# A fifteen-product scheme for the first matmul, with all orders of work laid out anew

## The chip, the cores and the metric

The kernel runs on one core of a Trainium2 chip. The metric is the time on the device, in microseconds (us), from launch to end. Every figure in the profile comes from one profiled execution. PE is TensorE's matmul, PEld its weight load, DVE is VectorE, ACT ScalarE, POOL GpSimd, SP SyncE, whose queue starts most DMAs.

## What is computed

An attention block with a decaying state (RWKV-6) for 4 batches, 8 heads, 768 steps and head size 48, and on its output a two-layer network with an exact gelu:

```python
for t in range(S):
    cur = np.einsum('bhd,bhe->bhde', u[None] * kt, vt)
    y[:, :, t] = np.einsum('bhd,bhde->bhe', rt, state + cur)
    state = wt[:, :, :, None] * state + np.einsum('bhd,bhe->bhde', kt, vt)
...
x = attn_out.transpose(0, 2, 1, 3).reshape(B * S, H * D)   # 3072 x 384
h = x @ w_in                                               # w_in 384 x 2048
g = 0.5 * h * (1.0 + erf(h * inv_sqrt2))
return g @ w_out                                           # w_out 2048 x 384
```

All of it is float32 on the chip.

## The kernel before

**Tiles.** The 3072 rows are worked in eight tiles of 384 (half a sequence of one batch). For tile x, `attention(x)` leaves the transposed rows in `xT` (128 partitions x 3 chunks of d_model x 384 tokens), and `mlp(x)` makes h, the gelu and the output from it. While `mlp(x-1)` runs, attention x is finished and attention x+1 begun. Attention's matmuls are 64x64 and come in bursts; its masks, products and states are DVE's, its copies into `a_sb` ACT's.

**Who sets the order.** Nothing is scheduled by a tool: the program is recorded in the order in which it is written out, and each engine works its own instructions in that order. Two tables hold the order. `PLAN[x]` is a string with a letter per step: "." is the next step of `mlp(x-1)`, "s" of attention x, "f" of attention x+1, "l" of the loads, "c" of the conversion of the weights, "w" of sums of weights, "x" of sums of tokens. `ORDER[x]` lists the steps inside `mlp(x)` for tiles 1 to 7. Tile 0 is computed plainly (`h_plain`, `g_plain`; lines 1121 and 1133), since the sums of weights are not there yet.

**The first matmul before.** h has 16 blocks of 128 rows, 3 chunks of d_model and 2 halves of 192 tokens: plainly 96 products of 128x128 by 192 columns. `h_ops` takes four steps q, each with four row blocks (2 from each half of h). Letters A to G add products into a PSUM bank (`two`, line 1043 issues them), with sums of weights (`s(1)` to `s(4)`) and of tokens (`t1` to `t4`, `l01`). Chunks 0 and 1 take seven products where eight would be plain, chunk 2 goes plainly. Small letters read a bank: "a" copies it into a second one (line 1091), "b", "d", "i", "j" are gelus (1072), "e", "f" copies into `g` (1104, 1106), "c", "g" saves into `o_sb` (1076), "k", "l" add a save to `g`, by an accumulating DMA from POOL's queue (1081) or for the last q by DVE (1083). The sums of weights are in `h_sums` (lines 1010 to 1018, in two parts, during tiles 0 and 1), those of tokens in `sums_of_x` (line 1029, five per tile).

**The second matmul**, `g_ops`, takes twenty products of four 128x128 by 192 each ("=" in the order), with sums of g by DVE ("+", line 1157), banks filled with zeros by ACT ("<", 1167) and ends ("!") by ACT (1188) or DVE (1190); the last ones store the rows. The change leaves its tables as they are.

**PSUM.** From tile 1 on, the first matmul has four banks: two of the tag "mm" (`bank`, `h_ps`) and two of "u" (`bank_u`, `u_ps`); attention has two pairs of banks (`pair`). A matmul that adds to a bank must wait until ACT has read it.

**Loads and conversion.** The weights come as float64 and are made float32 by ACT (lines 432 to 435) and DVE (440, 443). `rkw` comes through SP's queue.

Of the kernel before, what the change touches and what calls it, by code (L numbers as in the profile page):

```python
# [10 lines left out]
F32 = mybir.dt.float32  # L11
# [10 lines left out]
C = 64  # L22
G = 64
D = 48
# [16 lines left out]
        ".lls.....sslsc.lsslll.sl.sls..sl.lscsl..sss.lscs.lscs.s.clll.s..s.cccsss...wss..ss.ff"  # L41
    ),
    1: (
        "c.ccc.clccs.cc..csscc...wcsc.csc.s.c.ccsc.scl..c..csclwccs.ccc.sc.cccs..ccs.c..csss.c...s.ccss.scl.l"
        "wccc..ll.csccl.ccclcc.cfc.cwfwf..wcw.sfff...ff.w....lww.fff.fsfx.xfx..w.w.....w.f..f.cw.f..xx.."
    ),
    2: (
        "ss.w.s.sswssw.s.s....s...slsl.s.s.sw..ww.ss.w..sw...sw.ss..w......swws.ss..s.s..s.sss.l.wsw..s..ss.."
        ".s..l....ls.w..sw..s...w.s....ss.ssww.s..w.s...s.s.s..s.sl.s.......s.s.l........s..ls.s......s...l.."
        "f...ls...f..ff....fx.xx....ff.xffx"  # L50
    ),
    3: (
        ".................l...l...ss..s..ss...s.lsss..s..sss.s.s.sss..s..s.s.s......s.ss.ss.ss..s..ss.sss..ss"
        ".ss.s....l.sl..ss.....s.......ss.s.s..ss..s.s.ss..s.s...s......s.s...l....ssss..l..s.s.l..s.ls.f...f"
        "......lfxx.xx..x"
    ),
    4: (
        ".s.ss.l.......s.s............s....sl..s....sssss..s.ss..ss..s..ss......s.s..ssss..ss.sl..s..s..s.s.s"
        "s.s.....s.ss.ssss..ss.s.lss..ss.s..s.....s.s.l.s.s......sss.....ss.....ss..s...s.ssl..s..s...llsls.f"
        "....s.....f.l..fxx.xxx"  # L60
    ),
    5: (
        "...ss..ss.s..ss....s..s................l..ss.l.....s.slss.ss...s.ss.s....ss.s..s...sssss.sss..ss..s."
        "s....s...ssss.sss..s...ssss....s....ssss...s....sls.sssss..s..s........l.....s.....s..ssls..sl..ls.l"
        ".sf....f.f.f...lxxxx.x."
    ),
    6: (
        "...s...s.s.ss.s...s............l.s.....s...ss...ss....s.ss.s..ss..ssslss...s.s...ss.s.s...l.s.sl..ss"
        "s.s...s.s.ss..ss.s.s.sss..s.s...ss..s.ssss..sss...l..s...s.s..ss.s..........s....sl......ss.ls.l.lfs"
        ".s.ff.f....f..l..xx.xfffffffxx"  # L70
    ),
    7: (
        "........................s.s....sssss.s......sss.ss...ss.s...ssss..ss..s.s...ss.ss.....s..s.ss.s..s.s"
        "ss.s...s....s..s......s.s......s.....s..ss.ssss..s.ssss...s........s..s.s.s.s.s....s.......xx....xxx"
    ),
}

# [22 lines left out]
        "E0 e0 A0 a0 C0 c0 F0 B0 A1 b0 a1 E1 B1 F1 f0 e1 f1 k0 G0 G1 b1 g0 D0 A2 d0 a2 C1 l0 B2 g1 i0 c1 E2 e2 F2 "  # L100
        "C2 D1 j0 b2 l1 c2 d1 A3 k1 f2 G2 a3 g2 j1 k2 l2 i1 E3 e3 F3 f3 D2 C3 +22 c3 G3 g3 B3 =a +e5 D3 d2 <i l3 "
        "b3 d3 <g j3 j2 k3 i2 i3 +23 +03 +e0 =i =b +e1 =g =j +01 +e2 =k !b !k !g +e3 !a +E2 +E3 =h !j =c =m !h "
        "+00 =q !m +20 !c <p +E0 +e4 !q =l +E4 =n !l !n =s =p =o !s !p =f =t !f !o =r !t =d =e !r !d !i !e"
    ),
    2: (
        "A0 E0 a0 B0 F0 e0 b0 C0 A1 f0 a1 c0 G0 B1 g0 F1 E1 b1 f1 D0 e1 k0 C1 d0 !i c1 A2 a2 k1 G1 A3 i1 B2 g1 l0 "
        "b2 F2 i0 f2 D1 d1 a3 !b G2 j0 E2 l1 F3 B3 e2 C2 g2 b3 l2 c2 E3 j1 f3 G3 e3 C3 +22 g3 +e5 D2 l3 k2 j3 c3 "
        "d2 D3 i2 d3 =b j2 <g =a <i k3 +03 =g i3 =k =i +e0 +01 +00 +23 !k =j +e1 +e3 +20 !g =h !j +e2 +E3 +E2 =c "
        "!h !d =m +e4 !m !c =q <p +E0 =p =l !p !q =n !l +E4 !n =s !s =f =o !f =t =r !o !t =d =e !r !e !a"
    ),  # L110
    3: (
        "A0 E0 a0 B0 e0 b0 C0 A1 c0 F0 E1 a1 e1 f0 B1 b1 G0 A2 F1 g0 D0 C1 k0 l0 d0 f1 c1 a2 G1 F2 E2 g1 B2 k1 e2 "
        "D1 !a b2 f2 E3 d1 C2 e3 j0 c2 l1 A3 G2 a3 F3 j1 C3 k2 g2 !b i0 f3 D2 l2 d2 G3 g3 i1 D3 c3 k3 B3 <i l3 "
        "+22 d3 j3 b3 i3 j2 <g =i =a =g !d =b +03 =k i2 +23 +e0 +e5 !g +01 +e1 +e2 =j +e3 =h +E3 =c !k !h !j +00 "
        "!i +E2 =m +20 +E0 !m =q =l !q +e4 +E4 !l !c =n =s <p =p !s !p !n =o !o =f =t !f =r =d !t !r =e !e"
    ),
    4: (
        "A0 E0 a0 B0 e0 F0 b0 C0 f0 A1 G0 c0 E1 k0 a1 B1 g0 F1 e1 D0 b1 A2 l0 f1 C1 G1 d0 a2 g1 l1 B2 c1 b2 E2 D1 "
        "e2 F2 A3 f2 C2 j0 j1 d1 c2 a3 k1 k2 G2 F3 g2 i0 E3 f3 D2 i2 B3 e3 G3 l2 i1 g3 D3 d2 C3 b3 +22 <i l3 +e5 "
        "j2 j3 +e2 c3 d3 =i <g =b +03 +23 =g =a =k k3 !g =j +e0 i3 =h !d !k !j +01 !a =c +e1 +E2 +e3 +E3 !i +00 "  # L120
        "!h =m +20 !c !m +e4 =q <p !q =l +E0 !l +E4 =p =n =s !n !p !s =o !o !b =f =d !f =t =r !t !r =e !e"
    ),
    5: (
        "A0 E0 a0 F0 e0 B0 C0 b0 A1 f0 a1 G0 F1 g0 l0 f1 B1 c0 E1 e1 G1 b1 D0 C1 g1 k0 d0 A2 a2 c1 D1 !b E2 d1 B2 "
        "b2 l1 i0 F2 e2 C2 j0 k1 i1 c2 f2 A3 a3 G2 k2 F3 E3 g2 f3 D2 G3 d2 e3 l2 g3 j1 C3 i2 c3 B3 D3 +22 <i l3 "
        "!i k3 d3 =b <g j3 j2 +03 =g b3 +23 =i +e0 i3 !a =a +e5 +01 !g =k =h =j +e1 !k !j +e3 !h =c +e2 +E3 +E2 "
        "=m =q !c +00 !m !d +20 !q =l <p +e4 !l +E0 =p =n +E4 !p =s !n =o !s !o =t =f !f =d !t =r =e !r !e"
    ),
    6: (
        "A0 a0 E0 e0 F0 B0 C0 b0 A1 f0 G0 a1 c0 E1 B1 e1 k0 F1 C1 f1 c1 b1 G1 g0 k1 E2 A2 !a D0 d0 e2 g1 C2 l0 a2 "  # L130
        "c2 D1 d1 B2 A3 l1 b2 a3 F2 E3 f2 F3 !i j1 G2 i1 g2 B3 j0 f3 e3 !d i0 +22 D2 b3 l2 G3 +e5 +e2 k2 !b i2 g3 "
        "C3 D3 c3 l3 j3 d3 d2 <g =a =b j2 =g <i k3 +23 +03 +e0 i3 !g =k +01 =h +00 +E2 !k +e4 =i =c =j +e1 +E4 "
        "+20 !h =q +E0 !j +e3 +E3 !q !c =m !m <p =l =p !l =n =s !p !s !n =o =f !o !f =t !t =r =d =e !r !e"
    ),
    7: (
        "A0 a0 E0 e0 B0 b0 F0 f0 A1 a1 C0 c0 k0 G0 g0 l0 B1 b1 E1 e1 F1 f1 D0 d0 i0 A2 a2 j0 C1 c1 k1 G1 g1 l1 B2 "
        "b2 E2 e2 F2 f2 D1 d1 i1 A3 a3 j1 C2 c2 k2 G2 g2 l2 B3 b3 E3 e3 F3 f3 D2 d2 i2 G3 g3 l3 j2 C3 c3 k3 =a !a "
        "D3 d3 i3 j3 +22 +e5 =b !b <i +e2 =i !i <g +03 =g !g +23 +e0 +e1 =k !k +e3 +01 +E3 +E2 =j !j +00 =h !h "
        "+20 =c !c +e4 =m !m +E0 +E4 =q !q =l !l =n !n =s !s <p =p !p =f !f =o !o =t !t =r !r =d !d =e !e"
# [9 lines left out]
def kernel(  # L149
# [295 lines left out]

    xT_of, done, behind, ready = {}, set(), set(), set()

    def attention(x, unit):
# [14 lines left out]
        if x not in xT_of:  # L463
            xT_of[x] = wk.tile([128, NJ, T], F32, name="xT")
# [431 lines left out]
        for i in range(NI):  # L896
            for p in range(2):
                for b in range(np_):
                    q, c3 = divmod(i, N3)
                    for g in range(2):  # L900
                        c = 2 * c3 + (p + g) % 2
                        src, c0 = (st, c - 1) if c else (before, NC - 1)
                        if src is None:
                            continue
                        o = ((parts[b] * Q + q) * NC + c0) * D
                        nc.tensor.matmul(ys[b][0][c % 2][half[g ^ swap(b)], i * C:(i + 1) * C],  # L906
                                         lhsT=src[half[g], o:o + G], rhs=rc[half[g], b, i, c % 2],
                                         start=False, stop=True, skip_group_check=True)
        if split:
# [8 lines left out]
        for b in reversed(range(np_)):  # L918
            for q in reversed(range(Q)):
# [11 lines left out]
                ysb = wk.tile([128, T], F32, name="ysb", bufs=1)  # L931
# [48 lines left out]
    HK = HF // 2  # L980
    s_of, x_sums, s12_of = [], [], {}

    def homes():
# [9 lines left out]
        second = [more[1][:, i * WI:(i + 1) * WI] for i in range(HK)]  # L993
        third = [s_home[:, i * WI:(i + 1) * WI] for i in range(HK)]
        fourth = [z[:, FG * 128:] for z in spare]
        s_of.extend((second, third, fourth))

    def h_sums(k):

        if not k:  # L1000
            homes()

        def w(a, c, k):
            return w_in_sb[:, a * HK + k * 2:a * HK + k * 2 + 2, c, :]

        def pieces_of(i, k):
            return s_of[i - 2][2 * k:2 * k + 2]

        for i in range(2):
            nc.vector.tensor_sub(pieces_of(3, k)[i], w(0, 0, k)[:, i], w(1, 0, k)[:, i])  # L1010
        yield
        nc.vector.tensor_add(w(1, 0, k), w(1, 0, k), w(1, 1, k))
        yield
        for i in range(2):
            nc.vector.tensor_sub(pieces_of(2, k)[i], w(1, 0, k)[:, i], w(0, 0, k)[:, i])
        yield
        for i in range(2):
            nc.vector.tensor_sub(pieces_of(4, k)[i], w(0, 1, k)[:, i], pieces_of(2, k)[i])
        ready.add(k)
        yield  # L1020
# [301 lines left out]
```

## Time and profile before

| | us |
|---|---|
| median of 3 runs (583.15 to 585.53) | 585.1 |
| the profiled execution | 583.43 |
| its span, first to last instruction | 581.7 |
| first h product of tile 0 | 46.1 |
| first work of tile 1's part (banks cleared, L208) | 125.2 |
| first h product of tile 7 | 522.4 |

The windows below give us for the stretch, then the busy time of PE, PEld, DVE, ACT and POOL with the number of instructions, the granted clock, the share of DMA and its GB/s. The rows are ten-microsecond stretches of the start and of the turn from tile 0 to tile 1:

```profile
0.00:10.00 10.00, 7.68 (x114) 3.58 (x114) 5.27 (x29) 3.08 (x5) 5.10 (x16) 1.00 0.78 262
10.00:20.00 10.00, 6.51 (x246) 4.71 (x246) 9.79 (x22) 3.57 (x5) 2.86 (x5) 1.00 0.69 210
20.00:30.00 10.00, 8.27 (x233) 5.17 (x233) 7.70 (x16) 3.88 (x7) 0.00 (x0) 0.84 0.61 192
90.00:100.00 10.00, 10.00 (x81) 6.23 (x74) 9.36 (x29) 8.24 (x9) 0.00 (x0) 1.00 0.22 85
```

The groups of the profile give line, engine, operation, shapes and count, then the busy time, the mean time of one in ns, and how long the engine was idle before them. A float32 product is two matmul instructions. An instruction's own time includes the part in which the next one already runs, so the time that a product takes from PE is read from the distance of starts.

```profile
L1043 PE MATMUL h_ps<-xT,w_in_sb 128*128 128x192 f32 x560 | 109.7, 328 | 0.0
L1121 PE MATMUL h_ps<-xT,w_in_sb 128*128 128x384 f32 x96 | 33.2, 494 | 0.0
L1091 ACT COPY u_ps<-h_ps 128x384 f32<-128x384 f32 x28 | 13.1, 468 | 35.8 <-PE h_ps L1043 25.1
```

### The profile page before, as it was taken

The page shows a single profiled execution, that of the slowest core. Times are in us where ns is not written, and L with a number is a line of the kernel's source. Part 1 is how long each engine was busy: PE and PEld are TensorE (multiplying, and loading weights), DVE is VectorE, ACT ScalarE, POOL GpSimd, SP SyncE. Part 2 cuts the span into 40 slices and gives each one's busy share as a digit, 9 for nine tenths or more (in the row PEclk, how much of TensorE's full clock was granted, in tenths as well). Part 3 has the DMA queues.
Part 4 walks back from the last instruction along what each step waited for, and adds up shares of the span by engine and source line. Part 5 has one row for each costly group of instructions (what it writes and reads, how often), then busy time and mean ns, then how long its engine had stood idle before and what let it go on. Part 6 is the DMA issues. An engine that isn't in the chain of part 4 may idle for free.

```text
span 581.7 us, 17597 instructions
## 1 busy us (share of the span) xinstructions
PE 567.2 (98%) x7544; PEld 510.4 (88%) x7544; DVE 453.0 (78%) x880; ACT 290.2 (50%) x634; POOL 58.8 (10%) x63
## 2 busy tenths in 40 slices
PE   7789999999999999999999999999999999999997
PEld 3476666669999999999999999999999999999997
DVE  6878967989889978688887979789788988730171
ACT  2468987134762358235672357324671357425520
POOL 3100000003100030003100120003100021002200
PEclk9999999999999999999999999999999999999999
DMA  6669833222451442345223631526314242212401
GB/s 241 200 193 334 275 111 110 70 79 37 68 130 54 112 85 41 95 127 93 29 39 99 171 43 15 126 70 163 43 28 106 94 56 29 43 39 42 54 1 41
DMA packets 61853, 55.07 MB, mean 95 GB/s; under 512 B 32336, under 2 KB 46928, under 8 KB 61776
## 3 DMA queue, kind: packets, MB, share of 16 engines
q1 hardware_dynamic: 50256, 45.62, 26.1%
q0 software_dynamic: 11424, 8.26, 10.9%
q8 instruction: 59, 0.97, 0.7%
q14 instruction: 18, 0.15, 0.1%
q10 hardware_dynamic: 96, 0.07, 0.0%
HBM read 36.24 MB, written 4.72 MB: 70 GB/s over the span
## 4 chain that ended last, share of the span: by engine, by line
PE 94%; DVE 2%; DMA 1%; issue 1%; ACT 0%; SPq 0%; DVEq 0%
PE u_ps L1043 33%; PE h_ps L1043 19%; PE o_ps L1043 13%; PE h_ps L1121 6%; PE o_ps L1133 5%; PE d L689 5%; PE d L550 4%; PE kv_ps L817 2%; PE y_ps L906 2%; PE y_ps L859 2%; DMA rkw<-in_rkw_dram 1%; PE warm L324 1%; DVE st L833 1%; PE d L680 1%; DVE kx L487 1%
## 5 line engine op out<-in xcount | busy, mean ns | idle before, releaser
L1043 PE MATMUL h_ps<-xT,w_in_sb 128*128 128x192 f32 x560 | 109.7, 328 | 0.0
L1081 POOL DMA_DIRECT2D g<-o_sb x42 | 50.8, 1268 | 477.6 <-ACT o_sb L1076 296.9
L1043 PEld LDWEIGHTS h_ps<-xT,w_in_sb 128*128 128x128 f32 x560 | 93.3, 190 | 2.1 <-ACT u_ps L1091 0.8
L1043 PE MATMUL u_ps<-w_out_sb,g 128*128 128x192 f32 x224 | 41.8, 330 | 0.3 <-DVE g L1157 0.3
L1043 PE MATMUL u_ps<-s,w_in_sb 128*128 128x192 f32 x224 | 41.3, 328 | 0.0
L705 ACT COPY a_sb<-d 32x320 f32<-32x320 f32 (+5 forms) x108 | 39.1, 362 | 3.5 <-PE d L689 1.7
L1043 PE MATMUL o_ps<-t,g 128*128 128x192 f32 x224 | 40.0, 326 | 0.0
L1043 PEld LDWEIGHTS u_ps<-w_out_sb,g 128*128 128x128 f32 x224 | 36.7, 190 | 1.0 <-issue 0.5
L1043 PEld LDWEIGHTS u_ps<-s,w_in_sb 128*128 128x128 f32 x224 | 36.9, 190 | 0.6
L1043 PEld LDWEIGHTS o_ps<-t,g 128*128 128x128 f32 x224 | 37.0, 190 | 0.0
L1188 ACT ACTIVATE o_sb<-u_ps 128x192 f32<-128x192 f32 x21 | 6.9, 331 | 57.6 <-PE u_ps L1043 57.5
L833 DVE SCALAR_TENSOR_TENSOR st<-st,tot_sb,kv_ps 128x48 f32<-128x48 f32 x160 | 29.5, 259 | 7.7 <-PE kv_ps L817 7.7
L723 DVE COPY_PREDICATED a_sb<-quarter,d 128x480 f32<-128x480 uint8 (+5 forms) x54 | 23.2, 438 | 13.1 <-PE d L689 12.0
L1121 PE MATMUL h_ps<-xT,w_in_sb 128*128 128x384 f32 x96 | 33.2, 494 | 0.0
L1133 PE MATMUL o_ps<-w_out_sb,g 128*128 128x384 f32 x96 | 31.8, 489 | 0.0
L550 PEld LDWEIGHTS d<-rkw 64*64 64x64 f32 x1152 | 20.2, 140 | 12.9 <-issue 8.3
L1043 PE MATMUL u_ps<-w_extra,g 128*128 128x192 f32 x168 | 30.9, 328 | 0.3 <-ACT u_ps L1167 0.3
L1072 ACT ACTIVATE g<-g 128x384 f32<-128x384 f32 x56 | 28.2, 522 | 5.9 <-DMA g<-o_sb 3.9
L1091 ACT COPY u_ps<-h_ps 128x384 f32<-128x384 f32 x28 | 13.1, 468 | 35.8 <-PE h_ps L1043 25.1
L1157 DVE TENSOR_TENSOR g<-g 128x512 f32<-128x512 f32 x42 | 28.1, 682 | 3.4 <-ACT g L1072 3.1
L689 PE MATMUL d<-kx,rkw 64*64 64x96 f32 x1152 | 29.9, 247 | 0.0
L1083 DVE TENSOR_TENSOR g<-g,o_sb 128x384 f32<-128x384 f32 x14 | 7.5, 548 | 28.4 <-ACT o_sb L1076 28.4
(163 smaller groups left out, 1211.1 us busy)
## 6 DMA issues: line engine op xcount, KB each, us to landing
rkw<-in_rkw_dram SPq DMA_DIRECT2D x54, 256.0 KB, 3.5
g<-o_sb POOLq DMA_DIRECT2D x42, 192.0 KB, 3.6
raw<-in_w_out_dram SPq DMA_DIRECT2D x8, 768.0 KB, 7.7
v_in<-in_v_dram SPq DMA_DIRECT2D x8, 584.0 KB, 4.5
raw<-in_w_in_dram SPq DMA_DIRECT2D x5, 768.0 KB, 5.7
rkw<-kx SPq DMA_DIRECT2D x72, 48.0 KB, 2.0
out_dram<-o_sb SPq DMA_DIRECT2D x17, 192.0 KB, 1.9
rkw<-in_rkw_dram SPq DMA_DIRECT2D x6, 384.0 KB, 3.5
```

Source lines behind the costliest of these rows:

```text
L550: nc.tensor.matmul(d[half[p], g, n * width:(n + 1) * width], lhsT=kc[half[g], b, i, p], rhs=right(half[g], b, i, p), start=True, stop=True)
L689: nc.tensor.matmul(o[half[p], i * 3 * C // 2:(i + 1) * 3 * C // 2], lhsT=kc[half[g], n // NI, n % NI, p], rhs=rx[half[g], 2 * n + p], star ...
L705: nc.scalar.copy(out=at[z, g, first:behind, (a + 1) * h:], in_=d[z, :, :, to] if g == slice(None) else d[z, :, to])
L723: nc.vector.copy_predicated(out=an[:, :, :, :, (a + 1) * h:], mask=mask.to_broadcast(data.shape), data=data)
L833: nc.vector.scalar_tensor_tensor(out=stq[:, q, c], in0=stq[:, q, c - 1] if c else b4[:, q, NC - 1], scalar=totq[:, q, c:c + 1], in1=kvs[q ...
L1043: nc.tensor.matmul(o, lhsT=lhsT, rhs=rhs, start=start, stop=True, skip_group_check=True)
L1072: nc.scalar.activation(out=g_of(q, a, b), in_=z, func=AF.Gelu)
L1081: nc.gpsimd.dma_start(out=o, in_=z, accum_op=ALU.add)
L1091: nc.scalar.copy(out=u_of[q], in_=a_of[q])
L1121: nc.tensor.matmul(h_ps, lhsT=w_in_sb[:, f // FI, j, f % FI * 128:(f % FI + 1) * 128], rhs=xT[:, j, :], start=(j == 0), stop=(j == NJ - 1))
L1133: nc.tensor.matmul(o, lhsT=gs[f // FG][:, f % FG, i * 128:(i + 1) * 128], rhs=w_out_sb[:, f, :], start=(f == 0), stop=(f == NF - 1))
L1157: (nc.vector.tensor_add if op == "+" else nc.vector.tensor_sub)(*(a(i) for i in (z if z != "E0" else "20", x_, y_)))
```

## The change

Chunks, row blocks and token halves are taken together: three row blocks by three chunks by two token halves, eighteen products plainly, are computed with fifteen. `H_WEIGHTS` are 15 sums of weights, `H_TOKENS` ten of tokens, `H_PRODUCTS` names for each product its weights, its tokens, where its bank comes from ("new", the chain of another product, or a fresh bank filled with plus or minus another chain's content), and into which of six outputs it ends with what sign. Two rounds q = 0, 1 take six row blocks each (two at a time, in one bank of 384 columns); the last four row blocks (12 to 15) go plainly, with three products of 384 columns each ("p", "r").

In the order "*" is a product, "/" a bank filled from another, "e" the read of a bank at the end of a product, "k" the accumulating DMA, "i" the gelu of a finished sum.

```diff
+H_WEIGHTS = (
+    "12 12 - 22", "21 01 + 21", "x0 12 - 01", "12 02 - 12", "02 02 + 22", "x1 00 -- 20", "x2 00 + 12",
+    "x3 00 + 22", "22 01 + 22", "x4 11 - 21", "x5 10 + 22", "x5 x5 - 11", "11 x4 - 10", "20 20 + 11",
+    "10 10 + 12",
+)
+H_TOKENS = (
+    "s0 10 - 11", "s1 21 - s0", "s2 s1 - 20", "s3 s0 - 01", "s4 00 - s2", "s5 00 + s3", "s6 11 + 21",
+    "s7 20 + s5", "s8 01 + 11", "s9 01 - s4",
+)
+H_PRODUCTS = {
+    "A": "21 10 new .", "B": "22 s1 A .", "C": "x0 21 B .", "D": "x4 s8 C -5", "E": "11 s3 D +2",
+    "F": "x5 s0 E +3", "G": "20 01 F +5", "H": "12 s7 +C -2", "I": "x2 s9 H +1", "J": "01 s6 -B -5",
+    "K": "00 s4 J +1", "L": "x3 s2 K +0", "M": "x1 00 L -4", "N": "02 20 +A +0", "O": "10 s5 N +2",
+}
+H_BANKS = {"A": "m", "H": "u0", "J": "u1", "N": "u0"}
+H_ROUNDS = 2
+H_FIRST = {"0": "N", "1": "K", "2": "O", "5": "J"}
+H_BY_V = ("1G", "1L")
...
     7: (
-        "A0 a0 E0 e0 B0 b0 F0 f0 A1 a1 C0 c0 k0 G0 g0 l0 B1 b1 E1 e1 F1 f1 D0 d0 i0 A2 a2 j0 C1 c1 k1 G1 g1 l1 B2 "
...
+        "*A0 p12 r12 p13 /N0 *N0 r13 eN0 *B0 /J0 *O0 *C0 eO0 /H0 *J0 *D0 eJ0 eD0 *K0 *H0 eK0 eH0 *E0 *L0 p14 kD0 "
+        "eL0 kH0 r14 *M0 *I0 kL0 eE0 *A1 *F0 eM0 eI0 p15 kI0 /N1 kE0 i00 eF0 *N1 eN1 r15 *B1 *G0 /J1 +03 *O1 *C1 "
...
+    xT_bufs = [const.tile([128, NJ, T], F32, name=f"xT{i}") for i in range(2)]
...
-            xT_of[x] = wk.tile([128, NJ, T], F32, name="xT")
+            xT_of[x] = xT_bufs[x % 2]
...
+        assert x < 2 or h_is_done(x - 1)
...
-                ysb = wk.tile([128, T], F32, name="ysb", bufs=1)
+                ysb = wk.tile([128, T], F32, name="o_sb", bufs=3)
...
+    H_PLAIN = range(6 * H_ROUNDS, NF)
...
+    def h_sums(q):
+
+        assert h_is_done(0)
+        if not q:
+            homes()
+        for z in H_WEIGHTS:
+            o, a, op, b = z.split()
+            a, b = h_weight(q, a), h_weight(q, b)
+            o = h_weight(q, o)
...
+            yield
+
+    def tokens(x, z):
+        if z[0] != "s":
+            return xT_bufs[x % 2][:, int(z[0]), int(z[1]) * HT:(int(z[1]) + 1) * HT]
+        i = int(z[1])
+        return xT_bufs[(x + 1) % 2][:, i // 2, i % 2 * HT:(i % 2 + 1) * HT] if i < 6 else x_sums[i - 6]
...
+            def fill(q, p):
+                source = of_product[p][2]
+                assert held[q, chain_of[source[1]]] is not None
+                open_bank(q, p)
+                nc.scalar.activation(out=held[q, p][:, 0:2 * HT], in_=held[q, chain_of[source[1]]][:, 0:2 * HT], func=AF.Copy,
+                                     scale=1.0 if source[0] == "+" else -1.0)
+
+            def product(q, p):
+                w, z, source, _ = of_product[p]
...
                 for i in range(2):
...
+                    multiply(o[:, i * HT:(i + 1) * HT], h_weight(q, w)[:, i * 128:(i + 1) * 128], tokens(x, z), source == "new" and i == 0)
+
+            def end(q, p):
+                sign, m = of_product[p][3]
+                o, z = g_of(q, m), of_two(held[q, chain_of[p]])
+                scale = 1.0 if sign == "+" else -1.0
+                if len(inputs[m]) == 1:
+                    nc.scalar.activation(out=o, in_=z, func=AF.Gelu, scale=scale)
+                elif p == H_FIRST[m]:
+                    nc.scalar.activation(out=o, in_=z, func=AF.Copy, scale=scale)
+                elif f"{q}{p}" in H_BY_V:
+                    (nc.vector.tensor_add if sign == "+" else nc.vector.tensor_sub)(o, o, z)
                 else:
...
+                    saved[q, p] = wk.tile([128, DM], F32, name="o_sb", bufs=3)
+                    nc.scalar.activation(out=saved[q, p], in_=held[q, chain_of[p]][:, 0:2 * HT], func=AF.Copy, scale=scale)
...
+            def add(q, p):
+                m = of_product[p][3][1]
+                assert H_FIRST[m] in parts[q, m]
+                nc.gpsimd.dma_start(out=g_of(q, m), in_=of_two(saved[q, p]), accum_op=ALU.add)
...
+            def plain(f):
+                i = f - H_PLAIN[0]
+                held[f] = o = (bank("h_ps", 1) if i % 2 == 0 else bank_u(1))[:, 0:T]
+                for j in range(NJ):
+                    multiply(o, w_in_sb[:, f // FI, j, f % FI * 128:(f % FI + 1) * 128], xT[:, j], j == 0)
```

The chains share the four banks: A to G one of the "mm" banks (bank q), N, O and then H, I the first "u" bank, J to M the second; the plain blocks use the second "mm" bank and the second "u" bank in turn. Six of the ten sums of tokens lie in the xT of the tile before, so they can be made only when all h products of that tile are done, and attention x+1 may write its xT only when those of tile x are done. `o_sb` has three buffers in place of two and also serves for `ysb`. The sums of weights partly replace the weights in place. All strings of `PLAN` and all `ORDER` lists are new; the loads, the conversions, attention's steps and the second matmul's tables hold the same steps as before, at other places.

## The prediction

> **What bounds the kernel now.** I read the busy shares and the chain that ended last first, then one window per tile, then the last tile in order of time. From the page:
>
> ```profile
> PE 567.2 (98%) x7544; PEld 510.4 (88%) x7544; DVE 453.0 (78%) x880; ACT 290.2 (50%) x634; POOL 58.8 (10%) x63
> PEclk9999999999999999999999999999999999999999
> PE 94%; DVE 2%; DMA 1%; issue 1%; ACT 0%; SPq 0%; DVEq 0%
> ```
>
> PE holds 94% of the chain and its clock is full. Whether it is really full or only shown so is seen in the windows (us, then PE, PEld, DVE, ACT, POOL busy with counts, clock, DMA): tile 3, tile 5, and the last tile, which has no attention beside it.
>
> ```profile
> 256.30:322.60 66.30, 66.30 (x837) 63.86 (x837) 56.58 (x108) 32.80 (x80) 7.23 (x6) 1.00 0.37 83
> 389.70:455.60 65.90, 65.85 (x835) 63.34 (x834) 57.98 (x108) 32.52 (x80) 7.24 (x6) 1.00 0.39 85
> 522.40:578.40 56.00, 55.43 (x338) 54.41 (x336) 16.30 (x34) 19.22 (x45) 7.23 (x6) 1.00 0.21 39
> ```
>
> A tile takes 66 us, of which DVE works 57 and ACT 33. The timeline prices a product (start, length, line, count), and the third row shows how fast a bank is read out:
>
> ```profile
> 561.09 1.46 PE L1043 MATMUL u_ps<-w_extra,g 128*128 128x192 f32 x8
> 562.39 1.46 PE L1043 MATMUL o_ps<-w_out_sb,e 128*128 128x192 f32 x8
> ...
> 522.43 2.93 PE L1043 MATMUL h_ps<-xT,w_in_sb 128*128 128x192 f32 x16
> 523.28 0.46 ACT L1091 COPY u_ps<-h_ps 128x384 f32<-128x384 f32 x1 [5.34 <-DVE s L1029]
> ...
> 114.82 10.59 PE L1133 MATMUL o_ps<-w_out_sb,g 128*128 128x384 f32 x32
> ```
>
> Eight instructions in 1.30 us are 0.1625 us each. A product of 128x128 by 192 columns is two of them (the last tile has 336 for its 88 + 80 products): 0.325 us. The 384-column product is also two: (10.59 - 0.49)/31 = 0.326 us per instruction, 0.65 us. So PE time goes with columns; a wide product saves nothing. The row at 522.43 is 16 x 0.1625 + 0.33 long, so no gap lies in it, although B0, its third pair of products, waits for the copy at 523.28 that ends at 523.74; B0's place is 522.43 + 1.30 = 523.73. One pair (0.65 us) of cover just pays for one read of a bank, if ACT is free.
>
> **The change, part by part.**
>
> *Products.* Before, each of 4 steps q issues 2 x (1+2+2+2+1+1+2) = 22 narrow products: 88 per tile. After, two rounds of 15 x 2 = 60 narrow, and 4 plain blocks of 3 wide ones, worth 24: 84. Seven tiles lose 4 x 0.325 = 1.3 us each: **-9.1 us**. Against the eighteen of the plain form the new one drops much more, but the kernel before had already dropped 8 of 96.
>
> *ACT.* Before, 36 operations per tile (L1091 4, L1104 4, L1106 4, L1072 16, L1076 8), 17.5 us by their rows. After: 6 fills x 0.468, 8 gelus from a bank x 0.49, 8 first copies x 0.478, 10 saves x 0.48, 8 gelus of a finished sum x 0.522 = 19.5 us. They fall into a first-matmul part of 27.3 us of PE where it was 28.6; ACT alone has room (19.5 of 27.3 even without attention's products between).
>
> *Hand-overs.* What counts is the order. I took each of the 31 places per tile where a product reuses a bank that is being read, and counted the products between. In tiles 4 and 7 none has less than one pair; 8 and 7 have just one. In tiles 1, 2, 3, 5 and 6, 10 places have none in the written order; those of tile 1 that I followed in the built order have a burst of attention (1.9 us, as at 483.37) between. One pair is the cover that showed no gap, but in tile 7 three of the seven have another ACT operation ahead (C0, for example: its copy /J0 stands behind eN0; eN0 starts 0.2 after N0 ends, so /J0 is some 0.05 us late). The cost is unknown: lower end 0, upper end 0.48 us (one L1104 copy) at three places of each tile, 1.4 us. The trace before has gaps inside L1043 work of about 0.9 us per tile at similar cover, and keeps them. I take 0.35 per tile: **+2.5 us**, between 0 and 10.
>
> *Sums by accumulating DMA.* Ten per tile for six; POOL issues them in 1.27 us each, 12.7 us of a 65 us tile. Saves rotate over 3 buffers, not 2. In tile 7 the fourth save, eE0, needs the first, D0, to have landed: D0 is saved near 9.1 us into the tile, 3.6 to land (5.5 at worst), so 12.7, and E0's own turn comes at 13.7: nothing, and about 1 us if a landing is a slow one; it lies within the upper end above.
>
> ```profile
> L1081 POOL DMA_DIRECT2D g<-o_sb x42 | 50.8, 1268 | 477.6 <-ACT o_sb L1076 296.9
> L1072 ACT ACTIVATE g<-g 128x384 f32<-128x384 f32 x56 | 28.2, 522 | 5.9 <-DMA g<-o_sb 3.9
> ```
>
> *Token sums.* Ten for five, 0.28 us apart (0.39 where one needs the one before): +1.4 to 2 us of DVE per tile, hidden under its 9 idle us (66.3 - 56.6). Before, the last one ended 1.5 us into a tile. Now the first product that needs one (B0, s1) stands behind at least A0, p12 and N0 or p13: 0.65 + 1.94 + 0.65 = 3.2 us. Cost 0; without this cover it would be up to 2 us per tile. All now wait for the whole h of the tile before, since six lie in its xT; that ended half a tile earlier. The two adds by DVE replace two of L1083, 0.55 us each: 0.
>
> *Weight sums.* Thirty of 256 columns for 12 of 256 and 2 of 512. Back to back they start 0.33 us apart (0.60 the wide ones): 10.0 for 5.2 us, once. They lie where DVE is fullest, beside the end of tile 0 and the start of tile 1:
>
> ```profile
> 100.00:110.00 10.00, 10.00 (x123) 6.21 (x122) 9.83 (x20) 0.00 (x0) 0.00 (x0) 1.00 0.18 61
> 110.00:120.00 10.00, 10.00 (x123) 6.29 (x122) 9.90 (x12) 4.17 (x9) 0.00 (x0) 1.00 0.17 53
> ```
>
> Here PE could wait. Before, DVE runs from its state chain (90.11, L833) to the layout for attention's first burst (L664, ends 123.72): 33.6 us; the burst starts at 125.77, 35.7 after. In the new order this stretch holds 23 weight sums for 7 (+5.1), ten token sums for three (+2.0), two more passes of conversion (+2.2) and two masks (+0.2): 43.1 us. PE meanwhile has 35.7, plus three h products that moved behind the state chain (1.9), plus p12, A0, p13, B0 and N0 ahead of the burst (5.8): 43.4. So DVE is ready 0.3 us early, where it was 2 us early. I take **+0.5 us**; from 0 to 5 if waits that DVE shows elsewhere fall in here.
>
> *Start and the rest.* The loads, conversions and units of tile 0 and all slots of attention are laid anew. The same instructions stay, one conversion moves behind the states of tile 0, and the second unit's chain is split around a burst. The first 46 us are bound by loads and DVE, not by PE (0 to 30 us: PE 22.5 busy of 30, DVE 22.8). The nearest row for what this can move is one conversion pass with its multiply-out, 0.55 + 0.96 = 1.5 us, either way, more if a load is later: -2 to +3, taken as 0.
>
> *Sum.* The profiled run took 583.4 (span 581.7): 583.4 - 9.1 + 2.5 + 0.5 = **577.3 us**. It is 1.7 below the median of the three (585.1), whose scatter is 2.4; I predict 577.5.
>
> **The rivals.** A gain or loss of 0.5% is 2.9 us, about what measurement can tell here; "faster" means below 582.2.
>
> *Hand-overs eat the gain.* Fifteen products chained through four banks leave more reads between them than before (40 operations in 27 us). If the three places per tile with an ACT operation ahead each cost a whole copy, 7 x 1.4 = 10 us come back: 584. For it: ACT also carries attention's copies of 0.2 to 0.55 us (L705), which I did not place one by one. Against it: before, the same pattern showed no gap at 523.73.
>
> *PE was never the bound.* In the Trainium skill, "Perfetto Trace Analysis", section Identifying the Most-Contended Engine, the busy share of matmuls is called a poor measure of headroom and that of weight loads a better one; by it PE has 12% of the span free (PEld 88%). If that held in the tiles, removing products would leave the other waits where they are: 583 to 585. The windows speak against it: PEld is 96% and 97% busy in them, and starts follow each other at 0.1625 us. The missing share lies in the first 125 us, which the change does not shorten.
>
> *DVE becomes the bound from 90 us on (slower).* Between 90 and 190 us DVE is busy 91.4 us. The change adds 4.8 of weight sums, two rounds of token sums (3) and the moved conversions (2.2): 101.4. Its waits there, 8.6 us, are mostly for PE results and shrink if DVE is late; if they all stay, tile 2 begins 10 us late. If the lag is then carried, so that the tokens' 1.5 us come on top at five more turns, 7.5 more: 583.4 - 9.1 + 10 + 7.5 = 592. It decides from where the layout for the first burst of tile 1 ends later than B0 and N0 do, by more than some 9 us. Against it: tiles 2 to 6 leave DVE 9 to 12 idle us each to catch up.
>
> *The start gains and nothing new waits*: 583.4 - 9.1 - 2 = 572.
>
> **How the numbers follow.** The forecast, with its neighbours down to 572, gets 0.70; hand-overs that eat the gain 0.13, PE not the bound 0.04, both within 0.5%; DVE as the bound 0.13. The range goes from 571.5 (the best case) to 587 (past the cases without change; DVE's case is left out); the forecast's own range is 572 to 582. Faster 0.70, same 0.17, slower 0.13.
>
> **What would show it.** Per tile, PE should carry 280 narrow and 24 wide instructions in place of 336 narrow, and the last tile should take 54.7 to 55.5 us (56.0 before). Tiles 3 to 6 near 65.2. Gaps between products of the first matmul under ACT's fills and copies would show the hand-overs; a burst that waits for the layout (kx) after the first five products of tile 1 would show DVE. The forecast is wrong if tiles 2 to 6 don't get shorter by about 1 us each, or if the first tile-1 product starts more than 3 us away from 125.

## The result and the profile after

| | median | lowest to highest | runs |
|---|---|---|---|
| before | 582.9 us | 581.4 to 585.5 | 12 |
| after | 579.4 us | 577.9 to 582.6 | 12 |

The ratio is 0.9949, with a 95% interval of 0.9932 to 0.9966: 3.0 us faster, between 2.0 and 4.0. So the gain is shown, but whether it is more than the 0.5% that the prediction took as the least that can be told isn't: 0.5% lies inside the interval. The profiled execution took 578.3 us (583.4 before). Its page:

```profile
PE 562.7 (98%) x7306; PEld 478.3 (83%) x7320; DVE 463.9 (80%) x931; ACT 302.7 (52%) x662; POOL 93.0 (16%) x91
PEclk9989999999999999999999999999999999999999
```

PE is as full as before with 238 records fewer, and its clock is full but for a dip near the start. (The chain of waits is of no use in this profile: it has two stretches of 40 us put down to "issue", because a few matmul records are missing.) The windows of tiles 3, 5 and of the last one (us, then PE, PEld, DVE, ACT, POOL busy with counts, clock, DMA):

```profile
254.94:320.60 65.66, 65.61 (x803) 58.43 (x801) 57.24 (x111) 34.57 (x84) 12.07 (x10) 1.00 0.47 96
386.81:452.89 66.08, 65.53 (x802) 58.53 (x801) 57.24 (x112) 34.31 (x84) 12.13 (x10) 1.00 0.46 97
518.56:573.30 54.74, 54.45 (x305) 49.70 (x304) 17.57 (x40) 20.89 (x49) 12.13 (x10) 1.00 0.32 50
```

The last tile lost 1.3 us (it was 56.0), the full price of four products. The tiles in the middle lost little. From first product to first product in the two traces:

| tile | 1 | 2 | 3 | 4 | 5 | 6 | 7 | sum |
|---|---|---|---|---|---|---|---|---|
| before | 65.6 | 66.4 | 65.7 | 67.3 | 65.8 | 65.9 | 55.9 | 452.5 |
| after | 65.2 | 65.7 | 65.7 | 66.2 | 66.1 | 65.7 | 54.6 | 449.1 |

(Tile 1 of before is counted from its first burst of attention, which stood ahead of its first product.) Instead of 9.1 us the tiles lost 3.4. To find the rest I took the start of every matmul of the multiply line and subtracted what its predecessor needs (0.1625 us, or 0.323 us for one of 384 columns). What is left over is of two kinds, added up over the seven tiles:

| us | waits between products | refills: 0.104 on the second instruction | both |
|---|---|---|---|
| before | 1.6 | 5.3 (51 times) | 6.9 |
| after | 5.8 | 7.7 (74 times) | 13.5 |

A refill (my word; the rows don't show what happens in it) comes after nearly every wait, and after every return from a burst of attention: the first instruction starts, and the second comes 0.104 us later than its place. So -9.1 + 6.6 = -2.5 us was to be expected of the tiles, against the -3.4 that they show; some 0.3 us of the rest are the 168 wide instructions at 0.323 instead of 0.325 us, the other 0.6 aren't accounted for. The count doesn't see a wait that stands directly behind a burst of attention.

How one such wait looks is seen in the last tile. The timeline of PE and ACT in after (start, length, engine, line, operation, operands, count, and in brackets the idle time before it with what ended it):

```profile
523.99 0.49 ACT L1141 ACTIVATE g<-u_ps 128x384 f32<-128x384 f32 x1 [0.22 <-PE u_ps L1092]
524.53 0.92 PE L1092 MATMUL u_ps<-xT,w_in_sb 128*128 128x192 f32 x4
524.63 0.47 ACT L1122 ACTIVATE u_ps<-h_ps 128x384 f32<-128x384 f32 x1
525.28 0.81 PE L1092 MATMUL h_ps<-xT,s 128*128 128x192 f32 x4
525.49 0.49 ACT L1141 ACTIVATE g<-u_ps 128x384 f32<-128x384 f32 x1 [0.38 <-PE u_ps L1092]
525.93 0.81 PE L1092 MATMUL u_ps<-s,w_in_sb 128*128 128x192 f32 x4
526.20 0.47 ACT L1122 ACTIVATE u_ps<-h_ps 128x384 f32<-128x384 f32 x1 [0.22 <-PE h_ps L1092]
526.72 0.92 PE L1092 MATMUL h_ps<-s,s_home 128*128 128x192 f32 x4
```

The row at 525.28 is C0 (the digit is the round), and the one at 525.93 is J0. C0's last instruction ends its turn at 525.93. The fill /H0 reads C0's bank at 526.20, 0.27 us later, and ends at 526.67. D0 starts at 526.72, 0.05 us later again. J0 alone was to cover this: 0.65 us, to 526.58. So a fill under one pair of cover comes 0.79 - 0.65 = 0.14 us late, although ACT was free (0.22 us idle before it). And D0's four instructions are 0.92 us long instead of 0.81: the refill. O0 at 524.53 shows the same for a read by a first copy (at 523.99, with B0 between); the copy at 525.49 starts somewhat sooner after its product, 0.21 us. One such hand-over costs 0.09 to 0.15 us of wait and 0.10 of refill, about a quarter of a microsecond, with nothing out of order anywhere.

Two groups of after answer to those of before, the fills (42 for 28) and the gelus of finished sums (line, engine, operation, operands, count, then busy us and mean ns, then idle time before it and what ended it):

```profile
L1122 ACT ACTIVATE u_ps<-h_ps 128x384 f32<-128x384 f32 x42 | 20.1, 479 | 32.5 <-PE h_ps L1092 31.6
L1157 ACT ACTIVATE g<-g 128x384 f32<-128x384 f32 x56 | 28.2, 520 | 7.3 <-DMA g<-o_sb 5.9
```

The second column of times in the last row, and this row of the waits of after (engine, line, for what: us in total, times, longest us), say how long ACT stood for the landings:

```profile
ACT g L1157 <- DMA g<-o_sb: 5.9, 8, 1.3
```

ACT stands 5.9 us ahead of gelus for landings of accumulating DMAs in the whole execution (3.9 before). By the same view it stands another 5.1 us ahead of saves, whose buffer a landing frees (0.9 before). Ahead of 22 of the 42 fills it stands for the product that it is to copy, 31.6 us in all: for those it is early, not late.

### The profile page after: what moved, and what is told of

It reads as the page before. It is cut to its first block, busy times and chain, and to the rows that moved or that the text cites. A ratio compares the mean times of both kernels' runs of the same rounds, so it can differ in the third digit from the quotient of the medians.

```text
span 576.5 us, 17267 instructions
## 1 busy us (share of the span) xinstructions
PE 562.7 (98%) x7306; PEld 478.3 (83%) x7320; DVE 463.9 (80%) x931; ACT 302.7 (52%) x662; POOL 93.0 (16%) x91
## 4 chain that ended last, share of the span: by engine, by line
PE 78%; issue 15%; DMA 3%; DVE 1%; ACT 1%; POOL 0%; SPq 0%; DVEq 0%; POOLq 0%; ACTq 0%
PE u_ps L1092 28%; PE h_ps L1092 13%; PE o_ps L1092 11%; PE h_ps L1180 6%; PE o_ps L1194 6%; PE d L725 4%; PE d L586 4%; DMA g<-o_sb 2%; PE y_ps L942 2%; PE kv_ps L853 2%; PE y_ps L895 2%; DMA rkw<-in_rkw_dram 1%; PE warm L359 1%; PE d L716 1%; PE kt_ps L823 1%
## 5 line engine op out<-in xcount | busy, mean ns | idle before, releaser
L1153 POOL DMA_DIRECT2D g<-o_sb x70 | 85.0, 1381 | 446.8 <-ACT o_sb L1146 385.7
L1092 PE MATMUL h_ps<-xT,w_in_sb 128*128 128x192 f32 (+1 forms) x308 | 73.9, 373 | 0.3 <-ACT u_ps L1122 0.3
L1092 PE MATMUL u_ps<-xT,w_in_sb 128*128 128x192 f32 (+1 forms) x252 | 63.5, 384 | 0.0
L1092 PEld LDWEIGHTS h_ps<-xT,w_in_sb 128*128 128x128 f32 x308 | 53.1, 190 | 12.0 <-ACT u_ps L1122 0.5
L1092 PEld LDWEIGHTS u_ps<-xT,w_in_sb 128*128 128x128 f32 x252 | 43.6, 190 | 13.3 <-ACT g L1141 1.4
L1122 ACT ACTIVATE u_ps<-h_ps 128x384 f32<-128x384 f32 x42 | 20.1, 479 | 32.5 <-PE h_ps L1092 31.6
L1141 ACT ACTIVATE g<-u_ps 128x384 f32<-128x384 f32 x56 | 27.5, 490 | 17.6 <-PE u_ps L1092 16.2
L725 PEld LDWEIGHTS d<-kx,rkw 64*64 64x64 f32 x1152 | 24.9, 133 | 5.4 <-issue 4.2
L1194 PEld LDWEIGHTS o_ps<-w_out_sb,g 128*128 128x128 f32 x96 | 17.9, 190 | 12.9 <-ACT g L1185 0.6
```

The costliest lines, as they stand in the source:

```text
L725: nc.tensor.matmul(o[half[p], i * 3 * C // 2:(i + 1) * 3 * C // 2], lhsT=kc[half[g], n // NI, n % NI, p], rhs=rx[half[g], 2 * n + p], star ...
L1092: nc.tensor.matmul(o, lhsT=lhsT, rhs=rhs, start=start, stop=True, skip_group_check=True)
L1141: nc.scalar.activation(out=o, in_=z, func=AF.Copy, scale=scale)
L1153: nc.gpsimd.dma_start(out=g_of(q, m), in_=of_two(saved[q, p]), accum_op=ALU.add)
L1194: nc.tensor.matmul(o, lhsT=gs[f // FG][:, f % FG, i * 128:(i + 1) * 128], rhs=w_out_sb[:, f, :], start=(f == 0), stop=(f == NF - 1))
```

## The experiments

What I wanted to tell apart: the gain was lost in the hand-overs of banks (theory 1), or in the accumulating DMAs, or it was never to be had because something else sets the pace of tiles 2 to 6. All figures that follow are sums from the traces, by the same count as above:

| us | tiles 2 to 6, mean | last tile | waits | refills | ratio to before (95%) |
|---|---|---|---|---|---|
| before | 66.2 | 55.9 | 1.6 | 5.3 | 1 |
| before, four products fewer | 65.5 | 54.6 | 3.6 | 5.7 | 0.9897 (0.9871 to 0.9922) |
| after | 65.9 | 54.6 | 5.8 | 7.7 | 0.9949 (0.9932 to 0.9966) |
| after, once more | 65.9 | 54.9 | 5.9 | 7.9 | 0.9942 (0.9921 to 0.9964) |
| after without fills | 65.0 | 54.3 | 1.7 | 6.0 | 0.9867 (0.9844 to 0.9889) |
| after without accumulating DMAs | 65.5 | 54.6 | 4.4 | 7.4 | 0.9928 (0.9900 to 0.9955) |
| before with the new start | 66.2 | 55.9 | 1.5 | 5.4 | 1.0038 (1.0024 to 1.0053) |
| after, lists moved widely | 73.3 | 57.8 | 44.3 | 8.0 | 1.0805 (1.0777 to 1.0833) |
| after, lists moved a little | 65.7 | 54.8 | 3.9 | 7.1 | 0.9959 (0.9944 to 0.9975) |

**Four products fewer in before.** In steps 0 and 1 one of the two pairs of products of step B is left out, so the products are as many as in after, and nothing else moves.

```
-  "B": lambda q: two(a_of[q], q, (w(0, 1), x10), (w(0, 2), l0)),
+  "B": lambda q: two(a_of[q], q, (w(0, 1), x10), *([(w(0, 2), l0)] if q > 1 else [])),
```

> The kernel before, with the l0 part of step B left out for q = 0 and 1: four narrow products per tile fewer in tiles 1 to 7, at the same places, everything else as it was (those parts of h are missing from the output). It prices the step 'products' alone. Theory 1 (a product is worth 0.325 us wherever it stands; the change lost its gain in waits at the hand-over of banks): 9.1 us less than before, about 574 where before is 583. Rival (the orders around it don't give a removed product back in full, since DVE's attention chain or other waits fill the tile): 3 to 5 us less, as the change itself.

It became 6.0 us faster (1 - 0.9897 of 582; 4.5 to 7.5 by the interval): between the two expectations. The last tile got the whole 1.3 us, tiles 2 to 6 got 0.7 each. Waits grew by 2.0 and refills by 0.4 though no read was added, so a product that is left out seems to have been cover for a read as well; what each new wait stands for isn't worked out. Even without any new hand-over the 9.1 us of products were not to be had in full.

```profile
319.58:385.54 65.96, 65.20 (x842) 62.16 (x841) 57.31 (x111) 32.91 (x80) 7.23 (x6) 1.00 0.36 83
516.80:571.40 54.60, 54.13 (x330) 53.12 (x328) 16.18 (x34) 19.23 (x45) 7.20 (x6) 1.00 0.21 35
```

These windows of its tiles 4 and 7 show that PE still sets the pace: 65.2 of 65.96 us and 54.1 of 54.6 busy.

**No fills.** In after, the six fills of a tile's chains are left out and those chains begin on a fresh bank. This leaves out the copies and the parts of the sums that they carry over.

```
 def fill(q, p):
     open_bank(q, p)
-    nc.scalar.activation(out=held[q, p]..., in_=held[q, chain_of[source[1]]]..., func=AF.Copy, ...)
...
-    multiply(o[...], ..., tokens(x, z), source == "new" and i == 0)
+    multiply(o[...], ..., tokens(x, z), (source == "new" or source[0] in "+-") and i == 0)
```

> The changed kernel, with N, H and J started in fresh banks: the six ACT copies per tile that fill a bank from another are left out (the part of the sum that they carry over is missing). Each of them held up two banks. Theory 1 (hand-overs): the gaps inside the first matmul fall from about 2 us per tile to 1.2 or so, and the time by 4 to 6 us against the changed kernel, to about 574. Rival (accumulating DMAs): 0 to 1 us less, since no DMA changes. Rival (DVE): 0, DVE does the same work.

0.9867 against 0.9949 is 4.8 us faster than after, as theory 1 expected. Waits fell from 5.8 to 1.7 and refills from 7.7 to 6.0: 5.8 us, and the tiles got 5.3 us shorter with the same number of products. The window of the last tile, where nothing but the two multiplications runs:

```profile
516.35:570.59 54.24, 54.06 (x305) 49.73 (x303) 17.41 (x40) 18.22 (x43) 12.13 (x10) 1.00 0.32 49
```

and the start of its first multiplication there, in the timeline of PE:

```profile
522.23 0.92 PE L1092 MATMUL u_ps<-xT,w_in_sb 128*128 128x192 f32 x4
522.99 0.81 PE L1092 MATMUL h_ps<-xT,s 128*128 128x192 f32 x4
523.64 0.81 PE L1092 MATMUL u_ps<-s,w_in_sb 128*128 128x192 f32 x4
524.29 0.81 PE L1092 MATMUL h_ps<-s,s_home 128*128 128x192 f32 x4
```

C0, J0 and D0 (522.99, 523.64, 524.29) now follow each other at 0.65 us; O0 ahead of them still pays its read and refill (0.92). The comparison goes through the kernel before, which ran beside each of the two; the two intervals lie apart. What this run can't tell is how much of the 4.8 us is the fills as reads of a bank and how much is ACT's 18 us less work for other reads.

**No accumulating DMAs.** The ten adds of a tile are left out; the saves that fed them stay.

```
 def add(q, p):
     ...
-    nc.gpsimd.dma_start(out=g_of(q, m), in_=of_two(saved[q, p]), accum_op=ALU.add)
```

> The changed kernel without its ten accumulating DMAs per tile (the saved parts are never added). ACT no longer waits for a landing, neither before a gelu nor before it reuses a save buffer. Rival (accumulating DMAs late): 4 to 6 us less than the changed kernel. Theory 1 (hand-overs): 0 to 2 us less, by the two or three longest single waits of 0.5 to 0.7 us, which stand behind a landing.

1.2 us faster than after by the ratios (0.9928 to 0.9949), whose intervals overlap. In the trace three waits vanish: M0 in tile 5 (0.70 us) and a product of the second matmul in tiles 2 and 3 (0.49 and 0.21 us), 1.4 in all, which is the whole drop of the waits from 5.8 to 4.4. The waits of 0.09 to 0.15 us stay, and so does the one of 0.60 us at D1 in tile 4. ACT's 11.0 us of standing for landings are gone altogether, and PE gained 1.4 by it. The rival falls; DMAs have a share of about 1 us.

**The new start alone.** The kernel before with the new order of tile 0.

```
 PLAN = {
     0: (
-        ".lls.....sslsc.lsslll.sl.sls..sl.lscsl..sss.lscs.lscs.s.clll.s..s.cccsss...wss..ss.ff"
+        "l.l.l.ls.s..sssssss...s.sss.s..lclssll...sls.sls.lss..sl..lscl.cs.sc.sclls.sl.ffw.ccc"
```

> The kernel before with the new string for tile 0's start (PLAN[0]) alone. In the two profiles the work up to the first burst of tile 1 stands 1.7 us earlier after the change. If that is the new start, this kernel is 1.7 us faster than before and its first h product with its burst is done 1.7 us earlier; if it was chance of the loads, no difference.

Neither: it is 2.2 us slower (0.0038, interval 0.0024 to 0.0053), and in its profile the first product of tile 1 starts at 129.8 where it was 127.6. So the earlier start that the profile of after shows can't be put down to this order alone. Why this kernel is slower isn't shown. In its profile the granted clock is 0.50 from 37.6 to 47.8 us, where the profile of before has 1.00, and PE is busy 5.8 of the 6 us from 42 to 48: at full clock that would be half, so up to 2.9 us by this estimate, enough for the whole loss in that one execution. In the profiles of after and of its variants, whose code up to tile 1 is the same but for what the variant leaves out, the first product stands at 124.1 and 124.7 (after, twice), 123.3 (without DMAs), 126.8 (without fills), 126.2 and 128.0 (lists moved a little, and widely). Where I compared them with after instruction by instruction (without fills, without DMAs, lists moved a little) their difference arises before 55 us, while loads are landing, and stays from there to tile 1. A part of it is the clock. Without fills and with the lists moved a little, the granted clock is 0.50 for 3.4 us from 42.4 and from 42.0 us on, and in this stretch the same matmuls fall 1.2 us further behind those of after (from 1.65 to 2.80 us, and from 1.02 to 2.24). Without DMAs the clock is 1.00 all along there. What decides the rest, and when the clock falls, I haven't settled.

**Wider cover, by hand-over.** With four figures from the timeline above (a read starts 0.21 us after its product, a fill 0.27; each takes 0.47; PE goes on 0.05 later; each wait adds 0.104) I wrote a small sum over the lists, and it names the places of the waits in after nearly one by one. Then I let it permute the lists until most banks had two pairs of products between.

```
 ORDER = {
     2: (
-        "*A0 p12 /N0 *N0 *B0 eN0 r12 p13 r13 *O0 /J0 eO0 p14 *C0 /H0 *J0 eJ0 *D0 *K0 *H0 eD0 r14 eK0 eH0 kD0 *E0 "
+        "*A0 p13 /N0 *B0 p12 r13 *N0 /J0 *J0 r12 eN0 *C0 *O0 eJ0 p14 eO0 /H0 *D0 *H0 r14 eD0 *K0 *A1 eH0 kD0 *I0 "
...
```

> The kernel after with the same products, reads, fills, adds and interleaving letters; only the seven token lists are permuted, so that (by a small sum: a read starts 0.21 us after its product, a fill 0.27, each takes 0.47, TensorE resumes 0.05 later, and each wait adds 0.104) nearly every bank has two pairs, 1.3 us, of other products between a product and the next one that needs its bank, where the lists of after often have one. The sum, which names 27 of the 31 waits of after's tiles by their products, gives 7.4 us of hand-over waits over the seven tiles for the lists of after and 2.3 us for these. Theory 1 (the missing gain is hand-overs covered by one pair only): 3 to 5 us faster than after, about 574 to 577, waits inside the stream of products in the trace down from 5.8 to about 2 us, refills from 7.7 to about 6. Rival (removed waits come back elsewhere, as in the kernel before without four products, because DVE or the attention work sets the pace of tiles 2 to 6): within 1.5 us of after, and only the last tile shorter, by about 0.5 us.

> The kernel after unchanged, so that it and the permuted lists are compared on one chip in one session: both theories 0.994 to 0.997 of the kernel before.

The miss of the study: 8% slower, while after itself came out at 0.9942 again. Many of the hand-overs that were aimed at are gone (D0, O1 and H1 in tile 2, for example), but new waits of 0.5 to 6 us took their place. Two rows of its waits, PE's and ACT's:

```profile
PE u_ps L1092 <- ACT u_ps L1228: 11.7, 4, 6.3
ACT g L1157 <- DMA g<-o_sb: 22.3, 7, 6.2
```

and ACT and PE in tile 2, in the timeline:

```profile
230.99 0.50 ACT L1139 ACTIVATE g<-h_ps 128x384 f32<-128x384 f32 x1
237.69 0.52 ACT L1157 ACTIVATE g<-g 128x384 f32<-128x384 f32 x1 [6.20 <-DMA g<-o_sb]
238.12 0.31 ACT L1228 CAST u_ps<-zeros 128x192 f32<-128x192 bf16 x1
238.48 2.93 PE L1092 MATMUL u_ps<-w_out_sb,g 128*128 128x192 f32 x8 [6.31 <-ACT u_ps L1228]
```

The permutation had let saves, adds and gelus slide towards the second multiplication, and my sum priced no one who waits there. At 231.49 ACT is free, the next in its queue is the gelu of a finished sum, and the DMA that finishes it lands at 237.7. Behind the gelu stands the zeroing of a bank (L1228), and behind that PE's second multiplication. One late add in an in-order queue costs 6 us, as much as some 25 of the hand-overs that were mended. In after the same gelus wait 5.9 us in eight places, never more than 1.3.

**A little wider.** The same sum, but no gelu, add or DVE sum may come more than 0.8 us later than in after. It moves some 45 tokens of tiles 1 to 6 by a few places.

```
     2: (
-        "*A0 p12 /N0 *N0 *B0 eN0 r12 p13 r13 *O0 /J0 eO0 p14 *C0 /H0 *J0 eJ0 *D0 *K0 *H0 eD0 r14 eK0 eH0 kD0 *E0 "
+        "*A0 p12 /N0 *N0 *B0 eN0 r12 p13 r13 *O0 /J0 eO0 p14 *C0 *J0 r14 /H0 eJ0 *A1 *D0 *K0 *H0 eD0 eK0 eH0 *E0 "
...
```

> The kernel after with some 45 tokens of tiles 1 to 6 moved by a few places each (tile 7 stays), and with no gelu, no accumulating DMA and no add of VectorE let later than 0.8 us by the small sum, since the wide permutation of the experiment before let those go late and lost 50 us by it. The small sum names hand-over waits of 4.5 us for these lists against 7.4 for those of after. Theory 1 (hand-overs with one pair of cover cost the missing gain): 1.5 to 3 us faster than after, 0.989 to 0.992 of the kernel before, and the named waits (D1 and G1 in tile 1; O1, H1, F1 in tile 2; C1 and the plain block 15 in tile 3; E1 in tile 5; H1 and G1 in tile 6) gone from the trace. Rival (the lists of after are set by something else, and moving a few products only moves the waits): within 1 us of after, 0.993 to 0.997, with new waits of the same sum elsewhere.

Most of the named waits went: G1 in tile 1, O1 and H1 in tile 2, C1 and block 15 in tile 3, E1 in tile 5. D1 in tile 1 fell from 0.24 to 0.14, H1 in tile 6 stayed; F1 in tile 2 and G1 in tile 6 have no wait in after either. New are C1 in tile 4 with 0.33 us and small ones at M1 in tile 1 and D1 in tile 2. M0 in tile 5 fell from 1.00 to 0.07. Waits are 3.9 us for the 5.9 of after's second profile and refills 7.1 for 7.9. So 2.8 us of gaps went, but the tiles got only 1.4 us shorter (448.2 us for 449.6): tiles 2 and 5 gained, and tile 3 lost 0.4. There O1 waits 1.02 us directly behind a burst of attention, where the count doesn't look:

```profile
279.36 0.51 ACT L692 COPY kx<-rkw 128x384 f32<-128x384 f32 x1 [1.80 <-PE d L725]
279.78 0.48 ACT L1141 ACTIVATE g<-u_ps 128x384 f32<-128x384 f32 x1
280.32 0.92 PE L1092 MATMUL u_ps<-xT,w_in_sb 128*128 128x192 f32 x4 [1.02 <-ACT g L1141]
```

The list had moved the read eN1 (279.78) from ahead of B1 to behind it. With that it came behind attention's copy (279.36) in ACT's queue, which stands for the burst itself, and O1 needs the bank that eN1 reads. It is the mistake of the wide lists on a small scale.

The time is 580.2 us, 0.9959, and its interval overlaps that of after: no gain that can be measured. Its profile starts tile 1 at 126.2 instead of 124.7, which would eat what is left; 1.2 us of that is the stretch at half clock named above, in code ahead of all that this kernel changes, and whether its other runs had one isn't known. By time, the rival's figure came in, and one of the waits that it foretold; by the trace, theory 1 holds where the waits went, and the tiles gained just under its lower end.

## Why the prediction was right, and where it wasn't

The time (579.4 for 577.5) lay in the range, on the side that was forecast. But the sum forecast 6.1 us less (583.4 to 577.3), and the runs show 3.0, half of it. The two profiled executions lie 5.1 us apart, closer to the forecast; of this 3.4 us are the tiles and 1.7 the start, which moves from profile to profile, so that part is luck. Step by step:

- *Products, -9.1*: right. PE has 305 matmul records in the last tile's window (280 narrow and 24 wide were forecast), and that tile lost 1.3 us, four times 0.325.
- *Hand-overs, +2.5*: the mechanism was right, the size wasn't. It measured +6.6 us (waits 4.2, refills 2.4). The step that failed is the reading of the row at 522.43, "16 x 0.1625 + 0.33 long, so no gap lies in it". Sixteen instructions have fifteen distances: 15 x 0.1625 + 0.33 = 2.77, and the row is 2.93 long. There was a gap of 0.17 in it. It is B0, which waited 0.066 us for its copy and then paid a refill of 0.10. The weight load of B0 in the trace of before says so:

```profile
523.79 1.27 PEld L1043 LDWEIGHTS h_ps<-xT,w_in_sb 128*128 128x128 f32 x8 [0.20 <-ACT u_ps L1091]
```

  B0's place was 523.73. So one pair of cover doesn't pay for a read: 0.21 + 0.49 + 0.05 = 0.75 us by a copy that starts at once, 0.27 + 0.47 + 0.05 = 0.79 by a fill, against 0.65. Places with one pair, which I counted as free, are the bulk of the term: 25 of them wait 0.06 to 0.15 us in after, 3.0 us and 2.6 of refills, where before had eight with 0.6 and 0.8. The places where ACT has another operation ahead, which I priced, are few. And not all of the 6.6 are new hand-overs: with four products fewer in before, waits and refills grew by 2.4 without any new read.
- *Tiles 2 to 6 about 1 us shorter each*, the test that I set: not met, they got 0.35, so by its own sign the prediction's account of these tiles was wrong. That is the same error: before, their waits and refills were 0.85 + 4.15; after, 4.57 + 6.14. So 5.7 us of the 6.5 that they should have gained were given back, which leaves 0.16 per tile, and the rest of the 0.35 isn't accounted for.
- *DVE at the turn, +0.5*: the mechanism was right, and the cost came to nothing. Its state chain starts at 86.54 (90.11 before) and the layout that the first burst needs ends at 128.81: 42.3 us for the 43.1 that were worked out. The burst starts 43.4 us after the chain, as forecast; DVE was ready 1.2 us ahead of it, so it held nothing up. The rows of after, start and length first:

```profile
86.54 3.58 DVE L869 SCALAR_TENSOR_TENSOR st<-st,tot_sb,kv_ps 128x48 f32<-128x48 f32 x20
127.86 0.95 DVE L700 TENSOR_TENSOR kx<-kx,tot_sb 128x768 f32<-128x768 f32 x1
129.98 1.06 PE L725 MATMUL d<-kx,rkw 64*64 64x96 f32 x40
```

- *Accumulating DMAs, 0, at most 1 for a slow landing*: 1.4 us by the waits that vanish without them, 1.2 by time, which is not clear of noise: at its bound, or a little over. The places were others than the one worked out: M0 in tile 5 and two in the second multiplication, none in tile 7.
- *Token sums, 0*: B0 waits in no tile of after, so the cover held.
- *Start, 0 (-2 to +3)*: the first product of tile 1 lies at 124.1, but the variants show that it moves over nearly 5 us from kernel to kernel. The forecast's bound held in the profile of after; its middle was luck.

Of the rivals, *hand-overs eat the gain* came nearest: they took two thirds of it. Its mechanism, a whole copy of 0.48 us at three places per tile, was not what happened: in the last tile it was four places at 0.2 to 0.25, and in the others three to five such places with a longer wait among them in some. *PE was never the bound* fell: four products fewer and nothing else gave 6.0 us. The Trainium skill's rule in "Perfetto Trace Analysis", section Identifying the Most-Contended Engine, judges TensorE's headroom by the share of peak arithmetic and by the share of weight loads; here the latter fell from 88% to 83% (in the last tile from 97% to 91%) while the last tile stayed at 54.45 of 54.74 us busy and got shorter only by what was left out, so in this kernel the share of weight loads doesn't tell who sets the pace. *DVE as the bound* didn't happen.

## What to carry to other kernels

When instructions are taken off the engine that sets the pace, ask for each what else it did: here a product was also the cover for the read of another one's bank, and of 9 us removed 3 arrived. Price a hand-over between two engines from product to next product (0.75 to 0.79 us here), not by the length of the read (0.48), and count distances, not instructions, when a row is used to show that "no gap" lies in it. Before an order is mended at many small waits, look up what stands ahead of and behind each moved operation in its in-order queue: one late add cost more than all the small waits together, and one read that slid behind a copy of attention cost 1.0 us.

## What the runs showed of the hardware

- After nearly every wait, and after each return from a burst of small matmuls, the second multiply instruction comes 0.104 us late, 51 times in the tiles of before and 74 in those of after. The row with four instructions is then 0.92 us long for 0.81. These refills alone are 5.3 to 8.0 us of every kernel here.
- TensorE lost its clock after a pause of 6.3 us. The kernel with the widely moved lists, in tile 2, in windows as above:

```profile
224.00:231.00 7.00, 7.00 (x124) 6.31 (x123) 3.84 (x5) 6.19 (x17) 2.40 (x3) 1.00 0.37 49
238.40:241.60 3.20, 3.12 (x10) 3.12 (x11) 0.00 (x0) 1.48 (x5) 0.00 (x0) 0.50 0.46 79
```

  The clock is 1.00 before the pause and 0.50 after it; ten instructions take 3.12 us, nearly twice their 0.1625 each, and the clock is still 0.50 at 242.5. So a long wait is paid for twice, by some 2 us more here. The Trainium skill, "TensorE: Matmul & The Clock Gate", section Part 1: The HAM clock gate (the "warmup" mystery), has the clock halved after an idle window of about 3.4 us and restored after a busy one of the same length that runs free of the work. The trace agrees: the last matmul ahead of the pause ends at 232.2, the clock is 0.50 from 236.4 to 243.2, twice 3.4 us, and 4.7 us of that lie behind the pause.
- The same code under the same loads reached tile 1 between 123.3 and 128.0 us; in two of these profiles 1.2 us of it go with 3.4 us at half clock, from 42 us on.
